# Attention on two 64-row tiles of TensorE: unsplit fp32 scores, transposes in half blocks, a new order

## The chip, the cores and the metric

The kernel runs on one core of a Trainium2 chip. The metric is the device time of one execution in microseconds (us); before the change three runs took 736.19, 736.8 and 738.85 us, median 736.8.

## The reference, cut to what matters

```python
q_rot, k_rot = rotate(q), rotate(k)              # q, k, v: (2 batches, 8 heads, 576, 64), fp32
scores = q_rot @ k_rot.transpose(0, 1, 3, 2) / 8
attn = exp(scores - scores.max(-1))
attn = attn / (attn.sum(-1) + 1e-9)
x = (attn @ v) -> (1152 tokens, 512)
h = x @ w_in                                     # 512 x 2048
g = where(h >= 1, h, where(h <= -1, 0, (h + 1)**2 / 4))
x = g @ w_out                                    # 2048 x 512
p = domain_probs / domain_probs.sum(-1)          # 4 experts
out = sum over e of p[:, e] * (relu(x @ w1[e]) @ w2[e])   # 512 x 1024 x 512 each
```

`rotate` mixes the two 32-column halves of each head with cosines and sines of the position.

## The kernel before, in words

Three parts follow one another: attention, the first MoE layer (products at L654 and L708), the second (L910 and L947). The first layer's products start between the last heads' attention already. The change lies in the attention and in what is shared with it.

*Tiling.* `plan_pair` plans the attention eight times, each time for two heads of one batch. A pair has nine score tiles (`tile_step`): tiles 0 to 7 are a block of 128 queries of one head against that head's 576 keys, the ninth holds the last 64 queries of both heads, one in each half of the partitions.

*Keys and queries.* After the rotation (`rope`, on VectorE or GpSimd) each value x is split in two fp32r numbers, the rounded one h and the difference l (`split_h`, `split_l`). `tr` transposes blocks of 128 positions, h and l side by side, to 128 rows (64 of h, 64 of l); ScalarE copies them to `K1`, `Q1` and, for the ninth tile, `QT`. `K2` is K1 with the halves of the rows swapped, which two DMAs write (`swap`); the first pair has an opening of its own (`k_first`).

*A tile.* A score is Q1 times K1 plus Q1 times K2, for each half of the 576 keys: four matmuls of 288 columns into a two-bank tile `sc` of PSUM (L1300), in the ninth tile eight (L1310). VectorE takes the maximum (L1317), ScalarE the exponential with its sum into `E` (L1322). TensorE transposes four blocks of 128x128 into one bank `pt` (L1335), VectorE or ScalarE copies them to `PT` (L1281, L1283). The last 64 of the 576 keys, of both heads together, are transposed later (`tails`, L1361) and copied to `PU`.

*After four and after all nine tiles* the product with the values follows (`av`, L1411): unsplit fp32, two heads in the two 64-column halves of TensorE's array, five blocks of keys, 256 or 320 queries wide, into a bank of its own. An fp32 product leaves two records in the trace, so that the first four blocks show as x16 and the fifth as x4. Meanwhile the sums' reciprocals are transposed, copied (`rt`) and spread through DRAM by DMA; VectorE multiplies (L1422), and the result is split into `XH` and `XL` for the MoE part.

*PSUM.* Eight banks: two score tiles of two banks, three `pt`, which the transposes of keys and queries share, one `av`.

*What sets the order.* Each engine works through its instructions in the order in which `Plan.order` issues them. That takes the operations from a table, word by word,

```python
table = [self.ops[int(x)] for x in ORDER.split()]
```

and computes for each a start time by planned durations. Where TensorE would be idle for longer than `CFG["fill"]` by these, it inserts "warming" matmuls on a constant (`fill`, L1466), which compute nothing that is used.

Of the kernel before, what the change touches and what calls it, by code (L numbers as in the profile page):

```python
# [28 lines left out]
    "hd": [7, 7, 2, 2], "xd": [0, 3, 2, 2, 0, 3, 3, 2], "r0": 15, "xe": [2, 1, 3, 0, 3, 2, 2, 2], "he": [3, 2, 0, 3, 1, 0, 3, 0], "eb": 3, "rp": [239, 3, 33, 40, 240, 130, 40, 18], "ord0": [0, 1, 3, 5, 2, 4, 6, 7, 8], "ev": 204, "evu": 7, "fill": 272.0, "warm_to": 26000.0, "fill_to": 190000.0, "rule": 1.01, "tc": 190, "rkb": 1, "ahead": 42.6,  # L29
# [17 lines left out]
4 10 3 47 1 2 6 46 48 11 15 16 5 52 17 18 19 50 20 21 49 38 23 29 135 51 54 53 39 24 59 40 60 136 8 9 134 12 143 144  # L47
22 55 33 25 34 56 13 27 137 41 28 26 30 32 145 31 57 58 61 42 149 150 7 35 63 43 62 68 44 64 138 139 0 36 65 163 69 73
37 240 239 241 153 146 74 147 70 78 45 164 154 75 66 157 83 14 869 158 79 80 159 67 88 248 76 81 243 84 89 85 77 86 87
148 151 111 112 93 82 90 141 71 72 249 109 113 242 244 94 114 167 98 140 110 95 345 152 155 156 160 91 99 100 250 103  # L50
168 165 162 104 251 252 870 161 105 166 169 253 117 254 106 124 344 121 142 125 346 92 173 255 170 126 127 115 101 122
123 174 178 175 102 258 96 268 353 259 179 354 180 183 97 262 269 107 181 188 349 263 184 347 264 185 256 176 116 182
193 108 257 348 189 214 177 215 190 171 172 265 216 270 194 198 260 195 118 130 199 271 217 266 261 267 128 129 451
191 218 203 357 355 119 200 186 449 356 358 359 192 120 272 131 204 360 219 132 450 913 246 205 187 208 209 459 196
363 273 373 222 210 871 914 458 211 364 229 220 374 274 454 197 453 226 230 367 278 227 275 221 368 369 460 206 361
228 452 212 362 223 201 279 283 213 207 245 280 231 232 202 556 276 277 284 554 555 233 288 375 370 872 365 285 371
366 462 289 461 293 294 377 464 247 465 234 235 564 224 376 290 875 321 558 295 372 322 463 319 320 298 299 303 873
323 559 324 291 563 325 304 300 281 296 133 305 292 874 297 308 565 286 309 282 287 236 313 301 310 468 478 352 378
479 469 302 314 225 327 876 315 334 237 661 316 335 379 331 336 337 472 557 351 380 383 332 333 326 473 317 306 388
466 474 318 384 467 350 311 381 659 307 567 385 566 382 393 312 475 660 470 480 338 328 476 482 389 477 394 395 238  # L60
877 569 390 339 426 880 340 427 570 398 341 428 471 878 424 662 429 399 481 403 391 430 425 400 404 405 386 396 392
387 408 401 397 413 402 409 432 568 329 410 669 879 418 881 406 342 414 415 416 882 419 407 420 483 583 668 577 584
417 421 578 573 574 579 663 439 330 664 484 571 455 488 436 672 489 437 440 422 438 485 766 490 411 572 493 441 412
670 423 442 431 498 433 494 495 456 671 575 585 580 445 581 587 503 576 499 500 883 884 343 582 764 586 674 673 504
505 529 508 486 530 487 434 496 509 510 491 497 513 514 501 502 675 443 531 444 506 518 532 767 492 511 560 515 533
507 446 534 457 435 512 523 519 535 520 885 516 886 682 683 524 561 517 887 588 589 769 678 525 688 684 676 677 679
537 526 541 689 593 680 544 590 685 681 536 598 542 543 594 545 538 521 687 527 599 595 765 603 522 604 686 596 546
600 528 605 447 448 608 550 888 636 692 609 597 690 637 773 638 613 891 768 610 547 774 614 591 618 691 639 634 619
592 606 611 615 620 635 612 607 775 623 624 779 601 780 628 616 621 625 602 617 626 693 793 629 630 794 622 627 783
777 776 562 778 698 548 549 631 632 784 646 919 920 921 922 694 647 648 699 889 640 641 649 650 633 787 781 695 892  # L70
551 700 789 782 923 916 924 788 797 667 703 701 708 539 702 704 642 925 709 540 705 710 643 713 718 651 739 741 552
652 890 655 714 715 723 716 553 719 740 785 720 696 771 893 894 742 770 717 786 728 711 721 724 725 644 697 722 729
733 712 730 645 743 706 726 744 734 653 790 798 897 654 707 731 735 666 736 791 792 745 727 895 751 752 803 928 929
930 931 799 753 804 800 808 805 665 732 737 813 806 656 772 746 809 932 933 754 934 896 814 747 926 738 810 918 898
899 795 801 807 815 846 796 818 844 823 802 657 935 811 755 756 902 757 748 760 824 812 819 825 749 845 900 820 901
927 847 826 828 827 829 821 816 833 848 822 758 750 759 830 937 817 831 838 938 849 834 835 939 658 940 836 832 903
850 839 840 859 761 904 837 852 860 941 942 943 851 861 841 905 842 853 856 862 946 947 948 908 843 854 855 975 976
977 978 857 949 906 858 865 993 994 995 996 863 907 864 762 909 944 945 950 936 910 951 952 763 979 980 981 866 953
911 954 982 983 867 868 1011 1029 1012 1030 1031 1032 1087 1013 1014 1038 912 1039 917 1101 997 998 999 915 1020 1115
984 985 1040 1041 986 1015 1021 1042 1016 1022 1023 1017 1047 1048 987 1049 1000 1046 1001 1024 1028 1033 1034 1018  # L80
1035 1019 988 1025 1050 1036 1002 989 1003 990 1026 1004 1043 1005 991 1120 992 1006 1125 1027 1044 1088 1089 1007
1037 1076 1102 1008 1103 1045 1009 1116 1051 1117 1010 1056 1121 1057 1090 1077 1052 1104 1091 1058 1118 1105 1053
1122 1119 1059 1067 1054 1078 1068 1055 1069 1060 1070 955 1071 1079 956 1066 1072 957 1061 958 960 1073 959 961 1080
1062 962 1074 1064 963 1075 1086 965 1063 964 966 1065 967 1081 968 1092 1123 1093 970 969 971 1094 1082 972 1095 1084
973 1124 1083 1126 974 1085 1127 1096 1106 1128 1130 1129 1131 1107 1100 1132 1097 1133 1135 1108 1134 1136 1098 1109
1137 1138 1110 1140 1139 1141 1099 1114 1142 1143 1111 1145 1156 1157 1146 1144 1158 1112 1147 1159 1176 1148 1160
1177 1113 1161 1178 1179 1149 1185 1165 1186 1162 1155 1187 1180 1150 1188 1163 1181 1194 1189 1166 1195 1151 1164
1196 1153 1152 1197 1190 1239 1154 1198 1244 1167 1199 1249 1182 1254 1168 1183 1203 1191 1295 1204 1169 1205 1192
1206 1184 1175 1212 1170 1207 1213 1208 1214 1193 1171 1215 1200 1173 1240 1172 1201 1221 1174 1216 1222 1202 1217
# [105 lines left out]


def mm_ns(n):
    return max(86, n / 2.4 + 13.3)


T32, T32R = 109, 87


def act_ns(n, sbuf=False):
    return (93 if sbuf else 51) + 0.833 * n


# [1446 lines left out]
```

## Time and profile before

| | |
|---|---|
| median of three runs | 736.8 us |
| profiled execution | 736.78 us, span 735.0 us |
| TensorE (PE) busy | 726.4 us, 99% of the span |
| VectorE (DVE) busy | 536.5 us, 73% |
| ScalarE (ACT) busy | 351.4 us, 48% |
| GpSimd (POOL) busy | 90.0 us, 12% |
| granted clock of TensorE | 1.00 in all three stretches shown below |

The span is the recorded part of the execution. Busy is the time in which an engine has an instruction in work; matmuls are pipelined, so the records of neighbours overlap, and what a group of matmuls costs is read from the start of the first to the start of what follows.

### The profile page before, as it was taken

How to read it: one execution, taken by the hardware profiler on the slowest of the kernel's cores; microseconds unless marked ns; L12 is line 12 of the kernel's file. 1: busy time of each engine (PE TensorE's matmuls, PEld its weight loads, DVE VectorE, ACT ScalarE, POOL GpSimd, SP SyncE). 2: the span in 40 equal slices, each digit the busy share in tenths (PEclk: the TensorE clock that was granted, in tenths of full speed). 3: DMA queues.
4: the chain of work that ended last, by engine and by line, in shares of the span. 5: the costliest groups of instructions: out<-in, count | busy, mean ns of one | idle time of the engine just before them, and what ended most of it. 6: DMA issues, size and time to landing. Idle time of an engine off the chain costs nothing.

```text
span 735.0 us, 11809 instructions
## 1 busy us (share of the span) xinstructions
PE 726.4 (99%) x4545; PEld 663.3 (90%) x4545; DVE 536.5 (73%) x1054; ACT 351.4 (48%) x802; POOL 90.0 (12%) x88
## 2 busy tenths in 40 slices
PE   8999999999999999999999999999999999999998
PEld 6878788879999999999999988998889988999896
DVE  6789998899999843226898586774867849668462
ACT  4887798867776554335534232431324313333120
POOL 3764415000000112231200000000000000000000
PEclk9999999999999999999999999999999999999999
DMA  4545433325354200000111110111101110011002
GB/s 115 160 120 130 145 87 119 107 82 171 115 175 131 97 1 0 1 1 11 48 55 62 58 57 1 59 58 58 58 1 57 58 58 35 25 58 58 1 29 101
DMA packets 38872, 50.78 MB, mean 69 GB/s; under 512 B 7640, under 2 KB 22560, under 8 KB 38816
## 3 DMA queue, kind: packets, MB, share of 16 engines
q1 hardware_dynamic: 38126, 49.61, 21.9%
q8 instruction: 36, 0.59, 0.3%
q10 hardware_dynamic: 690, 0.41, 0.2%
q14 instruction: 20, 0.16, 0.1%
HBM read 43.26 MB, written 2.40 MB: 62 GB/s over the span
## 4 chain that ended last, share of the span: by engine, by line
PE 93%; DVE 3%; DMA 2%; ACT 1%; SPq 0%; issue 0%; POOL 0%; DVEq 0%; POOLq 0%
PE po L947 27%; PE q L910 23%; PE pi L654 14%; PE po L708 14%; PE av L1411 5%; PE sc L1300 4%; PE pt L1335 4%; PE sc L1310 1%; DMA rawk<-in_k_dram 1%; PE pu L1361 1%; DMA K<-K 1%; DVE tsa L919 1%; PE pstk L1183 1%; PE pstq L1183 1%; ACT E L1322 1%; DMA rbs<-rdram 0%
## 5 line engine op out<-in xcount | busy, mean ns | idle before, releaser
L919 DVE TENSOR_TENSOR tsa<-q,tsa 128x256 f32<-128x256 f32 (+1 forms) x224 | 93.7, 451 | 32.9 <-PE q L910 32.4
L947 PE MATMUL po<-w,ct 128*128 128x512 f32 (+1 forms) x328 | 99.2, 384 | 0.0
L962 DVE SCALAR_TENSOR_TENSOR ACC<-po,ptile,ACC 128x512 f32<-128x512 f32 (+1 forms) x64 | 46.9, 741 | 67.3 <-PE po L947 67.2
L947 PE MATMUL po<-w,hid1h 128*128 128x512 f32 x256 | 79.0, 390 | 0.0
L947 PEld LDWEIGHTS po<-w,ct 128*128 128x128 f32 x328 | 60.5, 188 | 11.7
L947 PE MATMUL po<-w,tsb 128*128 128x512 f32 (+1 forms) x164 | 63.0, 384 | 0.0
L1317 DVE TENSOR_REDUCE nm<-sc 128x1 f32<-128x576 f32 x72 | 53.8, 752 | 7.9 <-PE sc L1300 3.9
L1322 ACT ACTIVATE E<-sc,nm 128x576 f32<-128x576 f32 x72 | 53.6, 746 | 12.0 <-DVE nm L1317 8.9
L947 PEld LDWEIGHTS po<-w,hid1h 128*128 128x128 f32 x256 | 47.6, 188 | 9.4
L675 ACT ACTIVATE hb<-pi,half_t 128x384 f32<-128x384 f32 x48 | 27.7, 578 | 49.4 <-PE pi L654 49.4
L799 ACT CAST w<-wrawa 128x512 fp32r<-128x512 f32 x32 | 18.4, 617 | 67.0 <-PE po L947 64.7
L1300 PE MATMUL sc<-K,Q 128*128 128x288 f32 x256 | 49.3, 315 | 0.9 <-DMA K<-K 0.6
L947 PE MATMUL po<-w,hid1l 128*128 128x512 f32 x128 | 49.9, 390 | 0.0
L893 ACT ACTIVATE ct<-tsa 128x320 fp32r<-128x320 f32 x64 | 29.0, 471 | 42.9 <-DVE tsa L919 42.9
L679 DVE SCALAR_TENSOR_TENSOR hb<-hb,pi 128x384 f32<-128x384 f32 x48 | 26.3, 550 | 27.1 <-ACT hb L677 16.9
L893 ACT ACTIVATE hid1h<-tsa 128x256 fp32r<-128x256 f32 x64 | 25.4, 418 | 37.3 <-DVE tsa L919 37.3
L1335 PE MATMUL pt<-ident,E 128*128 128x128 f32 x288 | 40.1, 274 | 0.5 <-DVE PT L1281 0.3
L1300 PEld LDWEIGHTS sc<-K,Q 128*128 128x128 f32 x256 | 36.0, 188 | 4.7 <-issue 2.2
L922 ACT COPY tsa<-q 128x256 f32<-128x256 f32 (+1 forms) x32 | 12.7, 398 | 52.1 <-PE q L910 52.0
L720 DVE TENSOR_TENSOR ACC<-po,ACC 128x384 f32<-128x384 f32 x36 | 20.0, 555 | 23.9 <-PE po L708 23.9
L947 PEld LDWEIGHTS po<-w,tsb 128*128 128x128 f32 x164 | 30.8, 188 | 6.1
L1335 PEld LDWEIGHTS pt<-ident,E 128*128 128x128 f32 x288 | 33.1, 140 | 2.8 <-ACT E L1322 1.0
(234 smaller groups left out, 1961.4 us busy)
## 6 DMA issues: line engine op xcount, KB each, us to landing
wrawa<-in_moe_w_dram SPq DMA_DIRECT2D x16, 1024.0 KB
wrawa<-in_moe_w_in_dram SPq DMA_DIRECT2D x5, 1024.0 KB
wrawa<-in_moe_w_out_dram SPq DMA_DIRECT2D x5, 1024.0 KB
K<-K SPq DMA_DIRECT2D x14, 304.0 KB
ta<-in_moe_w_in_dram SPq DMA_DIRECT2D x3, 1024.0 KB
ta<-in_moe_w_out_dram SPq DMA_DIRECT2D x3, 1024.0 KB
rawk<-in_k_dram SPq DMA_DIRECT2D x16, 128.0 KB
RV<-in_v_dram SPq DMA_DIRECT2D x16, 128.0 KB
```

Of the source, the lines that this page charges most:

```text
L654: nc.tensor.matmul(ps()[:, 0:384], w[:, kt * P:(kt + 1) * P], x[:, kt, cols], start=(kt == 0 and m == 0), stop=(kt == 3 and m == 2))
L708: nc.tensor.matmul(ps()[:, 0:N], lh, rh, start=(kt == 0 and m == 0), stop=(kt == 3 and m == 2))
L893: op("ACT", act_ns(n, port) + 20, pr, lambda: nc.scalar.activation(hv(0), src(), AF.Relu), rk + gates[0], [hk], bufs, phase=1)
L910: nc.tensor.matmul(ps()[:, 0:n], w[x][:, kt, a * P:(a + 1) * P], r[y][:, kt, :], start=(kt == 0 and m == 0), stop=(kt == 1 and m == 2))
L919: nc.vector.tensor_tensor(ct(a, j), psv(), ct(a, i), op=ALU.add)
L947: nc.tensor.matmul(ps()[:, 0:f1 - f0], x[y], w[z][:, f0:f1], start=(kt == 0 and m == 0), stop=(kt == 3 and m == 2))
L962: op("DVE", 65 + 1.17 * (f1 - f0), pr, lambda acc=acc, ps=ps, t=t, f0=f0, f1=f1: nc.vector.scalar_tensor_tensor(acc(), ps()[:, 0:f1 - f0], ...
L1300: nc.tensor.matmul(sc()[:, a, 0:288], lh, KK()[:, c0:c0 + 288], start=(x == 0), stop=(x == 1))
L1317: op("DVE", 665, g0 + O["max"], lambda: nc.vector.tensor_reduce(nm(), pv(), axis=AX.XY, op=ALU.max, negate=True), [sc], [nm], [sc, nm])
L1322: nc.scalar.activation(Et()[:, o0:o0 + 576].rearrange("p (a c) -> p a c", a=2), pv(), AF.Exp, bias=nm(), scale=1.0, accum_out=sm()[:, s:s ...
L1335: nc.tensor.transpose(ps()[:, t * P:(t + 1) * P], Et()[:, c0 + t * P:c0 + (t + 1) * P], ident)
L1411: nc.tensor.matmul(pa()[64 * j:64 * j + 64, 0:N], lh, rh, start=(t == 0), stop=(t == 4))
```

## The change

*Scores.* Keys and queries are no longer split. A head has 64 dimensions, so a product needs only 64 rows of the array; keys 0 to 287 lie in the upper 64 rows (`KF`), keys 288 to 575 in the lower. A tile is two fp32 matmuls of 288 columns, one with the upper half of the rows into the first bank of `sc`, one with the lower half into the second (L1336); the ninth is four. Queries are needed in both halves of the rows: `QX` holds half of the blocks in each, and `QY`, written by DMA, the halves swapped (the DMA of keys goes). The first pair (`FB`) writes its queries twice instead.

*Transposes.* `turn` transposes a block as two halves of 64 rows, one from the upper rows into the first bank, one from the lower into the second. The target is the score tile itself, once its exponential has been read out. The last 64 keys are a fifth block of the second head's tiles (of both in the ninth); `tails` and `PU` go. So a score tile keeps its banks until its transposes are copied to `PT` (L1374, L1376, L1380). Keys and queries are transposed in the same way, in tiles of the same ring (`psk`, `psq`).

*PSUM.* Three score tiles, and two banks for `av`, the reciprocals' transposes and the MoE's first products; a third bank joins these when the attention is through (`psJ`).

*Waits and engines.* `av` also waits for `rt`. A string of bits (`alt`) says for about 190 operations whether VectorE or its alternative does them: copies on VectorE or ScalarE, rotations and differences on VectorE or GpSimd. VectorE has 9 copies of 512 and 12 of 640 elements of exponentials (32 of 512 before), ScalarE 23 of 512, 20 of 640 and the ninth tiles' seven (40 of 512 before).

*Order.* `ORDER` is a new table. On TensorE the scores are 128 matmuls of 288 columns and 32 on half as many stationary columns (256 and 64 before), the transposes 824 halves (483 full blocks before), the warming matmuls 31 (34), 15 of them after the first score (3); 72 matmuls of the MoE stand ahead of the last av (60).

```diff
 ORDER = """
-4 10 3 47 1 2 6 46 48 11 15 16 5 52 17 18 19 50 20 21 49 38 23 29 135 51 54 53 39 24 59 40 60 136 8 9 134 12 143 144
+4 1 16 0 3 15 17 2 19 18 10 29 28 11 5 20 38 34 30 33 22 24 119 35 39 21 6 31 44 23 7 9 36 114 43 113 32 40 25 8 37 26
...
-    psT = ctx.enter_context(tc.tile_pool(name="psT", bufs=3, space=PSUM))
+    psT = ctx.enter_context(tc.tile_pool(name="psT", bufs=2, space=PSUM))
-    psS = actx.enter_context(tc.tile_pool(name="psS", bufs=2, space=PSUM))
-    psA = actx.enter_context(tc.tile_pool(name="psA", bufs=1, space=PSUM))
+    psS = actx.enter_context(tc.tile_pool(name="psS", bufs=3, space=PSUM))
...
+        def turn(ps, e, t, zs=(0, 1)):
+            for z in zs:
+                r = slice(64 * z, 64 * z + 64)
+                nc.tensor.transpose(ps()[:, z, 64 * e:64 * e + 64], t[r, :], ident[r, r])
...
+        def both(t, e0, e1):
+            return t[:, :, 64 * e0:64 * e1].rearrange("p h (e c) -> p e h c", c=64)
...
+            def tq():
+                for e, z in enumerate((0, 5, 3, 7, 2)):
+                    turn(psq, e, R()[:, 576 + 64 * z:576 + 64 * z + P])
...
+            def swap():
+                for j in range(2):
+                    nc.sync.dma_start(QY()[64 * j:64 * j + 64, 0:640], QX()[64 - 64 * j:128 - 64 * j, 0:640])
...
+        def query(u, j, a):
+            r = slice(64 * a, 64 * a + 64)
...
+            c = (2 * j + u // 2) * P
+            return (QX if u % 2 == a else QY)()[r, c:c + P]
+        def keys(j, a):
+            return KF()[64 * a:64 * a + 64, 320 * j + 32 * a:320 * j + 32 * a + 288]
...
-                def qk():
-                    lh = Q1()[:, j * 512 + i * P:j * 512 + (i + 1) * P]
-                    for a in range(2):
-                        c0 = j * 576 + a * 288
-                        for x, KK in enumerate((K1, K2)):
-                            nc.tensor.matmul(sc()[:, a, 0:288], lh, KK()[:, c0:c0 + 288],
-                                             start=(x == 0), stop=(x == 1))
...
+            def qk():
+                for a in range(2):
+                    for jj in (j,) if s < 8 else (0, 1):
+                        o = sc()[:, a, 0:288] if s < 8 else sc()[64 * jj:64 * jj + 64, a, 0:288]
+                        nc.tensor.matmul(o, query(i, jj, a), keys(jj, a), start=True, stop=True)
...
             def tt():
-                for t in range(4):
-                    nc.tensor.transpose(ps()[:, t * P:(t + 1) * P], Et()[:, c0 + t * P:c0 + (t + 1) * P], ident)
+                for t in range(nb):
...
+                        c = 512 if t == 4 else 640 * j + t * P
+                        turn(sc, t, Et()[:, c:c + P])
...
+                    cp(PT[g]()[:, 4 * j:4 * j + nb, c:c + P].rearrange("p a (h c) -> p a h c", h=2), both(sc(), 0, nb))
...
-            pa = buf("av", f"av{n}{g}")
+            pa = buf("pt", f"av{n}{g}")
...
-            rk = [(PT[g], z) for z in range(lo, hi)] + [(PU[g], 0)]
+            rk = [(PT[g], z) for z in range(lo, hi)] + [rt]
```

Where the second pair's last tiles meet the third pair's first, TensorE had this before (a name is the buffer, with pair and tile: `pt1_5` is tile 5 of pair 1, counted from 0, `av10` pair 1, first product; `hlk3` are the split keys of pair 3):

```order
L1335 MATMUL pt1_5_731<-ident_58,E1_2_608 128x128 x4
L1183 MATMUL pstk3_0_736<-identr_59,hlk3_694 128x128 x4
L1300 MATMUL sc2_0_741<-K1_2_537,Q1_2_653 128x288
L1300 MATMUL sc2_0_741<-K2_2_699,Q1_2_653 128x288
...
L1183 MATMUL pstk3_8_746<-identr_59,hlk3_694 128x128
L1411 MATMUL av10_748<-PT01_590,RV1_94 64x256 x8
L1411 MATMUL av10_748<-PU01_606,RV1_94 64x256 x2
L1361 MATMUL pu1_1_784<-ident_58,E1_2_608 128x128
L1361 MATMUL pu1_1_784<-ident_58,E1_3_684 128x128
L1361 MATMUL pu1_1_784<-ident_58,E1_4_759 128x128
```

and has this now:

```order
L1336 MATMUL sc1_8_683<-KF1_335,QX1_370 64x288 x2
L1336 MATMUL sc1_8_683<-KF1_335,QY1_427 64x288 x2
L1336 MATMUL sc1_7_694<-KF1_335,QY1_427 128x288
L1336 MATMUL sc1_7_694<-KF1_335,QX1_370 128x288
L1336 MATMUL sc2_0_710<-KF2_691,QX2_592 128x288
L1336 MATMUL sc2_0_710<-KF2_691,QY2_616 128x288
L1425 MATMUL av10_716<-PT01_489,RV1_92 64x256 x10
L1362 MATMUL sc1_8_683<-ident_58,E8_90 128x64 x10
L1145 MATMUL sc1_7_694<-ident_58,E1_3_640 128x64 x10
L1403 MATMUL rb11_772<-ident_58,r11_748 5x128
L1145 MATMUL sc2_0_710<-ident_58,E2_0_740 128x64 x8
```

Scores of three tiles now stand together, then one av, then the three tiles' transposes into those same tiles; before, scores, transposes of another tile and transposes of keys alternated.

On ScalarE, shortly ahead of that place, exponentials (L1322) and copies stood in turn:

```order
L1322 ACTIVATE E1_2_608,sum1_499<-sc1_4_566,nm1_4_600 128x576
L1283 COPY PT01_590<-pt1_0_610 128x4x128
L1380 ACTIVATE r10_621<-sum1_499 128x2x2
L1322 ACTIVATE E1_2_608,sum1_499<-sc1_5_592,nm1_5_625 128x576
L1194 ACTIVATE Q1_2_653<-pstq2_8_623 128x128
L1202 ACTIVATE Q1_2_653<-pstq2_4_616 128x384
L1194 ACTIVATE Q1_2_653<-pstq2_0_632 128x512
```

Now they stand there so (L1349 is the exponential, L1374 the copy out of a score tile, `psk2` the transposed keys of pair 2):

```order
L1349 ACTIVATE E1_2_619,sum1_474<-sc1_5_595,nm1_5_613 128x576
L1349 ACTIVATE E1_2_619,sum1_474<-sc1_4_610,nm1_4_632 128x576
L1349 ACTIVATE E1_3_640,sum1_474<-sc1_6_598,nm1_6_635 128x576
L1374 COPY PT11_669<-sc1_5_595 128x5x128
L1374 COPY PT11_669<-sc1_4_610 128x4x128
L1161 COPY KF2_691<-psk2_672 128x256
L1163 COPY KF2_691<-psk2_672 128x64
...
L1349 ACTIVATE E8_90,sum1_474<-sc1_8_683,nm1_8_704 128x576
L1349 ACTIVATE E1_3_640,sum1_474<-sc1_7_694,nm1_7_708 128x576
L1349 ACTIVATE E2_0_740,sum2_741<-sc2_0_710,nm2_0_713 128x576
```

Three exponentials follow one another, then the copies of their tiles; the queries' copies of several sizes have gone from between.

## Rows read from the trace of the kernel before

**Rows 1.** The page: busy by engine (part 1), and the chain by engine (part 4).

```profile
PE 726.4 (99%) x4545; PEld 663.3 (90%) x4545; DVE 536.5 (73%) x1054; ACT 351.4 (48%) x802; POOL 90.0 (12%) x88
...
PE 93%; DVE 3%; DMA 2%; ACT 1%; SPq 0%; issue 0%; POOL 0%; DVEq 0%; POOLq 0%
```

**Rows 2.** Windows: stretch, its us, busy (count) by engine, PEclk, DMA share, GB/s.

```profile
0.00:15.00 15.00, 12.23 (x57) 9.61 (x58) 10.05 (x28) 5.05 (x13) 3.02 (x14) 1.00 0.40 115
15.00:167.20 152.20, 149.93 (x1179) 123.73 (x1178) 134.34 (x272) 124.45 (x350) 60.96 (x49) 1.00 0.43 118
167.20:735.00 567.80, 564.25 (x3312) 529.98 (x3312) 392.07 (x757) 221.86 (x441) 25.98 (x26) 1.00 0.16 55
```

**Rows 3.** Waits of TensorE, 15.0 to 167.2: us in all, times, longest.

```profile
PE pstk L1183 <- POOL hlk L1166: 0.9, 1, 0.9
```

**Rows 4.** Timeline of TensorE: start, us, instructions; 43 to 59, stage's first and last.

```profile
15.00 0.77 PE L1300 MATMUL sc<-K,Q 128*128 128x288 f32 x4
...
43.24 0.78 PE L1300 MATMUL sc<-K,Q 128*128 128x288 f32 x4
43.85 0.60 PE L1335 MATMUL pt<-ident,E 128*128 128x128 f32 x4
44.21 1.31 PE L1310 MATMUL sc<-K,QT 128*128 128x288 f32 x8
45.35 0.60 PE L1335 MATMUL pt<-ident,E 128*128 128x128 f32 x4
45.71 0.54 PE L1183 MATMUL pstk<-identr,hlk 128*128 128x128 f32 x4
46.09 0.76 PE L1300 MATMUL sc<-K,Q 128*128 128x288 f32 x4
...
46.83 1.95 PE L1411 MATMUL av<-PT,RV 128*64 128x256 f32 x16
...
49.14 0.55 PE L1361 MATMUL pu<-ident,E 128*128 128x128 f32 x3
...
50.41 1.47 PE L1335 MATMUL pt<-ident,E 128*128 128x128 f32 x12
51.64 0.77 PE L1300 MATMUL sc<-K,Q 128*128 128x288 f32 x4
...
55.72 2.38 PE L1411 MATMUL av<-PT,RV 128*64 128x320 f32 x16
...
58.56 0.44 PE L1361 MATMUL pu<-ident,E 128*128 128x128 f32 x2
...
166.46 0.71 PE L1411 MATMUL av<-PU,RV 128*64 128x320 f32 x4
```

**Rows 5.** Groups of VectorE by shape, 0 to 175: count, busy us, mean ns, idle before.

```profile
L1281 DVE COPY PT<-pt 128x512 f32<-128x512 f32 x32 | 21.4, 683 | 0.3
L1281 DVE COPY PU<-pu 128x320 f32<-128x320 f32 x8 | 3.9, 490 | 3.1 <-PE pu L1361 3.0
L1281 DVE COPY PU<-pu 128x256 f32<-128x256 f32 x8 | 3.3, 416 | 0.4 <-PE pu L1361 0.4
L1281 DVE COPY PU<-pu 64x64 f32<-64x64 f32 x8 | 1.8, 228 | 0.3
```

**Rows 6.** Groups of ScalarE by shape, 0 to 175.

```profile
L1283 ACT COPY PT<-pt 128x512 f32<-128x512 f32 x40 | 23.2, 587 | 7.2 <-PE pt L1335 7.1
L1188 ACT CAST K<-pstk 128x512 fp32r<-128x512 f32 x14 | 8.0, 583 | 0.1
L1194 ACT ACTIVATE Q<-pstq 128x512 fp32r<-128x512 f32 x8 | 4.8, 595 | 0.3 <-PE pstq L1183 0.2
```

**Rows 7.** Timeline of ScalarE: one exponential and the reading of its sum.

```profile
44.84 0.74 ACT L1322 ACTIVATE E<-sc,nm 128x576 f32<-128x576 f32 x1 [0.25 <-DVE nm L1317]
45.49 0.19 ACT L1322 ACTIVATION_READ_ACCUMULATOR E<-sc,nm 128x1 f32 x1
```

**Rows 8.** Timeline of TensorE in the opening: warming matmuls.

```profile
9.71 1.07 PE L1466 MATMUL warm<-identr 128*128 128x512 f32 x4
```

## What I expected, and why

> **What bounds the kernel now.** I read the page's busy shares and its chain first: TensorE is busy for 726.4 of 735.0 us, and 93% of the chain that ends last is TensorE's own work [rows 1]. Then the busy time by stage [rows 2]. The attention stage lies between 15.0 us, where the first score is issued, and 167.2 us, where the last product with the values ends [rows 4]. In these 152.2 us TensorE is busy 149.9 us, VectorE 134.3 (88%), ScalarE 124.5 (82%); the granted clock is 1.00, which is the upper of the two levels. What TensorE waits for in the stage comes to 2.3 us, and its longest waits are single ones of under 1 us [rows 3]. Behind the stage lie 567.8 us of the two MoE layers, again TensorE from end to end. Their matmuls are the same in number and shape before and after (576 + 576 + 1344 + 876 of the first layer's two products and the second's), so I cost that part at nothing. The start is costed at nothing too: the first score still follows the whole chain of the first pair's rotations on VectorE, some twenty small operations in either kernel. So the change is worth what it takes out of TensorE's stream in the attention stage, less the new gaps it leaves there.
>
> **The terms.** A "busy" of a matmul is no price, because the records of neighbours overlap; I use start to start in the timeline of 16 us in the stage [rows 4].
>
> *Scores.* A score tile of four 288-column matmuls runs from 43.24 to 43.85, 0.61 us, and the eight of the ninth tile from 44.21 to 45.35, 1.14 us. Eight pairs have 64 and 8 of these: 64 x 0.61 + 8 x 1.14 = 48.2 us. After, every tile is two (ninth: four) unsplit fp32 matmuls, which stand in the upper and the lower half of the array's rows and write two banks. No row shows that form. Nearest are the products with the values (av): unsplit fp32 too, two at a time in the two halves of the array's columns, in five steps. They take 46.83 to 49.14 = 2.31 us with 256 columns and 55.72 to 58.56 = 2.84 us with 320. The difference, 0.53 us over 5 x 64 columns, is 1.66 ns for a column of such a double step; what is left of 2.31 us, 0.19 us, is going into and out of the split array. So a score tile costs 288 x 1.66 = 0.48 us if halves of rows run beside each other as halves of columns do, and 0.96 if they don't. I take 0.48, since the av rows show the side-by-side running at these sizes: 72 x 0.48 = 34.4 us, **13.8 us less**.
>
> *Transposes.* Twelve full ones take 50.41 to 51.64, four 45.71 to 46.09: 0.095 us each. Before there are 288 of the exponentials, 40 of their tails and 129 of split keys and queries after 15 us (155 in all, 26 in the opening): 457 x 0.095 = 43.4 us. After, each becomes two half blocks; the tails ride along as a fifth block, and the keys and queries, no longer doubled by the split, need 10 halves each for a pair. That is 796 halves, 398 couples, after the first score. The price of a couple isn't in the trace. Side by side and in proportion to the columns it would be half a full one, 0.0475 us; side by side and at a fixed price for a block, 0.095; one behind the other, 0.19. I take 0.071, between the first two, because the rows lead there: a 288-column matmul of a score takes 0.61 / 4 = 0.1525 us, a 128-column transpose 0.095, so 160 columns cost 0.0575 us, 0.36 ns each, and 0.049 us are left as the fixed part; 64 columns then make 0.072. 398 x 0.071 = 28.3 us, **15.1 us less**.
>
> A rule speaks against it. The trace has 0.095 us for a full block [rows 4], and none for a half. The Trainium skill, page "TensorE: Matmul & The Clock Gate", section "LDWEIGHTS (loading the stationary operand)", says that loading the stationary block takes as long for few rows as for all, since its columns decide; the stationary block of a half transpose keeps its 128 columns. By that rule halving gains nothing as soon as the load decides; this is rival 4.
>
> *Changes between the whole and the split array.* Before, 31 (only av is split); after, 94 from the first score on, since scores and transposes are split one way, av another, and the small transposes of the sums and the MoE's matmuls not at all. At 0.19 / 2 = 0.095 us each, 63 more are **6.0 us more**. The same skill, page "TensorEngine Tiling (Array Packing)", section "Key Properties", has such a change drain the engine; the trace agrees as far as the 0.19 us of av go.
>
> *New waits.* The order now issues three score tiles in a row and their transposes in a row (the first pieces in the section on the change), because a tile's transposes go back into its own two banks and three such tiles are all there are. From a tile's start to the end of its exponential the trace has 43.24 to 45.58, the read of the sum to 45.68 [rows 4, 7]; that is 2.4 us in which TensorE needs other work. With an av (2.3 to 2.8 us) between the scores and the transposes it has it; one batch of three in each pair has none. I put 0.7 us on each of seven pairs, 5.0 us. In the first pair, 15 warming matmuls are placed after the first score where 3 were; they stand where nothing else was ready: 12 more at 0.22 us, from four in 9.71 to about 10.6 [rows 8], 2.6 us. Together **7.6 us more**; the bounds are 0 and 15.
>
> The av also waits now for the transposed sums' copy on ScalarE, and behind it on TensorE stand the next tiles' transposes; the sums' transpose is placed rows ahead of it, so I cost that at nothing, and at up to 0.3 us for each of 16 if it is late (in the bounds above).
>
> *VectorE and ScalarE* must not become the end. VectorE loses the second copies of tails, 3.3 + 3.9 + 1.8 us, the casts and differences of the split, some 7, about 3.4 of weight differences that go to GpSimd, and copies of exponentials (32 of 0.683 become 9 of that size and 12 of 640 elements at 0.82): about 24 us less [rows 5], 110 in the stage. ScalarE gains about 11 us of such copies and of the ninth tile's, and loses about 22 of key and query copies, casts and tails against it [rows 6]: some 114. TensorE is left with 149.9 - 13.8 - 15.1 + 6.0 = 127. So it remains the fullest, but no longer by far.
>
> **Sum:** -13.8 - 15.1 + 6.0 + 7.6 = -15.3 us. The profiled execution took 736.8 us, its span 735.0, and the median of the runs is 736.8 as well; the forecast is 721.5 us.
>
> **Rivals.**
>
> 1. *Half transposes run one behind the other.* Then a couple costs 0.19 us, 47.4 us more than I take, and 5 of the new waits vanish under it: 721.5 + 47.4 - 5 = 764 us, slower. The price decides from 0.071 + 15.3 / 398 = 0.11 us on. For it: no row shows halves of rows at work. Against: av's halves of columns overlap. If the scores ran one behind the other as well, another 34 us. This is the case on the other side.
> 2. *The ring of three score tiles is the bound.* A tile now holds its banks through exponential, transposes and copy. By rows, 2.4 us to the sum, 0.2 and 0.3 for the transposes, 0.6 to 0.7 for the copy: 3.6 us. But in a batch of three the second and third wait their turn for ScalarE, one exponential with its sum (0.85 us by the starts 44.84 and 45.68) more each: about 4.5 on average. With two further uses a pair of 1.5 us each, the stage lasts (72 x 4.5 + 16 x 1.5) / 3 = 116 us, under the 137 of the forecast (152.2 - 15.3). It would be the bound at 5.3 us, and at 6.0 the whole gain is gone. VectorE and ScalarE at above 80% make 5.6 possible: (72 x 5.6 + 24) / 3 = 142, 5 us more than forecast, and a few at the seams between pairs: 729 us.
> 3. *The clock.* TensorE, now waiting more often, falls from 2.4 to 1.2 GHz for part of the stage. For it: gaps of 1 to 2 us in a batch without av. Against: 1.00 in the opening as in the stage, waits included [rows 2]. A quarter of 127 us at half speed costs 32 us: about 753 us.
> 4. *A block's price is fixed.* Two halves side by side cost what one full block does, 0.095 us: 398 x 0.024 = 9.5 us more than I take, 731 us. For it: the fixed part above is already half of a block's price. Against: the other half goes with the columns.
>
> **How the numbers follow.** Forecast 0.51, rival 1 0.12, rival 2 0.14, rival 3 0.09, rival 4 0.14. The forecast's own range, by 0.0475 to 0.085 for a couple (-9 to +6 us), waits of 0 to 15 us, and up to 6 us on scores for loads that aren't covered, is 707 to 735. For 8 in 10, I go down to 704 and up to 741, which takes in rivals 2 and 4 and leaves out rival 1 and most of 3. A measurement of this kernel tells about 0.5% (3.7 us) from no change. Faster: nearly all of the forecast and of rivals 2 and 4, 0.77; same: their upper ends, 0.08; slower: rivals 1 and 3, 0.15.
>
> **What would show it.** In the profile after: the last av ends between 150 and 156 us, not at 167; a score tile start to start near 0.48 us and ten halves near 0.36; TensorE idle 5 to 15 us in the stage, most of it before transposes and released by ScalarE; the granted clock 1.00; the stretch from the last av to the end as long as before, or shorter by the 12 MoE matmuls more that now precede it. A tile at 0.9, ten halves at 0.9, or idle time released by the copies out of the score tile would show rivals 1 or 2 right. The forecast is wrong if the last av ends after 163 us, or if the MoE part grows.

## The result

The changed kernel takes 730.03 us in the median of six runs (726.69 to 730.6), the kernel before 736.36 in six of its own; the ratio is 0.9896 (95% interval 0.987 to 0.9923). That is 6.3 us less where 15.3 less was forecast: inside the range, the right sign, and less than half of the size. The profiled execution took 726.87 us, 9.9 less than that of before. Two of the six runs lie near 727 us and four near 730; what may part them is looked at with e4 and e5, and is not shown for all of them. The steps are first held against the profile.

The page of the changed kernel, parts 1 and 4, to be read beside [rows 1]:

```profile
PE 711.7 (98%) x4883; PEld 622.1 (86%) x4883; DVE 514.6 (71%) x1002; ACT 344.3 (47%) x763; POOL 89.5 (12%) x92
...
PE 90%; DVE 3%; ACT 2%; DMA 2%; SPq 1%; issue 1%; POOL 0%; DVEq 0%; POOLq 0%; ACTq 0%
```

Its windows, cut at the first score and behind the last av, columns as in [rows 2]:

```profile
0.00:10.76 10.76, 8.40 (x45) 5.40 (x46) 6.21 (x23) 4.31 (x13) 1.51 (x13) 1.00 0.47 129
10.76:158.90 148.14, 140.69 (x1546) 88.64 (x1542) 114.67 (x222) 119.08 (x313) 61.03 (x53) 1.00 0.39 109
158.90:725.10 566.20, 562.60 (x3302) 528.10 (x3300) 393.78 (x759) 220.90 (x439) 26.96 (x26) 1.00 0.16 55
```

The stage is only 4 us shorter (148.1 for 152.1, which is 15.00 to 167.10 by the starts; [rows 2] cut 0.1 us later), but begins 4.2 us earlier; behind it 566.2 us are left for 567.9, since 12 more MoE matmuls stand ahead. VectorE and ScalarE come to 115 and 119 us, 5 us more each than worked out (110, 114). TensorE's timeline in and around the second pair, to be read beside [rows 4]:

```profile
29.16 2.38 PE L1425 MATMUL av<-PT,RV 128*64 128x256 f32 x20
31.47 1.09 PE L1145 MATMUL sc<-ident,E 64*128 64x64 f32 x28
32.49 0.38 PE L1403 MATMUL rb<-ident,r 128*5 128x128 f32 x2
32.80 0.53 PE L1145 MATMUL psq<-ident,R 64*128 64x64 f32 x10
33.16 0.51 PE L1336 MATMUL sc<-KF,QX 64*128 64x288 f32 x1
...
34.82 2.91 PE L1425 MATMUL av<-PT,RV 128*64 128x320 f32 x20
37.66 0.53 PE L1145 MATMUL sc<-ident,E 64*128 64x64 f32 x10
...
49.56 0.47 PE L1145 MATMUL sc<-ident,E 64*128 64x64 f32 x10
49.87 0.46 PE L1336 MATMUL sc<-KF,QX 64*128 64x288 f32 x1
...
50.51 2.91 PE L1425 MATMUL av<-PT,RV 128*64 128x320 f32 x20
...
156.05 2.91 PE L1425 MATMUL av<-PT,RV 128*64 128x320 f32 x20
```

28 halves take 31.47 to 32.49, ten 32.80 to 33.16: 0.073 us a couple (forecast 0.071). Three score tiles ahead of an av take 33.16 to 34.82 = 1.66, so 0.55 each with the change into av; a batch of one takes 0.64 (49.87 to the av at 50.51), so each further tile costs 0.51 (forecast 0.48). Both prices hold. What doesn't is the time between. A batch of three tiles that has no av behind its scores, on TensorE:

```profile
45.17 0.51 PE L1336 MATMUL sc<-KF,QY 64*128 64x288 f32 x1
...
46.39 0.51 PE L1336 MATMUL sc<-KF,QX 64*128 64x288 f32 x1
...
47.66 0.46 PE L1145 MATMUL sc<-ident,E 64*128 64x64 f32 x8 [0.52 <-ACT E L1349]
48.38 0.53 PE L1145 MATMUL sc<-ident,E 64*128 64x64 f32 x10 [0.26 <-ACT E L1349]
```

and ScalarE in the same place, where L1374 is the copy that frees an older score tile:

```profile
45.76 0.57 ACT L1374 COPY PT<-sc 128x512 f32<-128x512 f32 x1
46.77 0.74 ACT L1349 ACTIVATE E<-sc,nm 128x576 f32<-128x576 f32 x1 [0.44 <-DVE nm L1344]
47.41 0.19 ACT L1349 ACTIVATION_READ_ACCUMULATOR E<-sc,nm 128x1 f32 x1
47.50 0.73 ACT L1349 ACTIVATE E<-sc,nm 128x576 f32<-128x576 f32 x1
```

The first tile starts at 45.17, its maximum follows, its exponential ends at 47.5 and its transposes start at 47.66: 2.5 us after the tile's start, of which the matmuls of the three tiles fill 1.5 (3 x 0.51). The third tile, at 46.39, also starts only when the copy of 45.76 has ended at 46.33: the ring of three has no tile to spare. Such waits stand only in part in the list of waits, for this stage:

```profile
PE sc L1145 <- ACT E L1349: 3.6, 10, 0.7
PE sc L1362 <- ACT E L1349: 0.8, 2, 0.6
PE sc L1336 <- ACT PT L1380: 0.7, 2, 0.4
```

so the rest is found by pricing: what the prices don't cover is put down to waits and warming, and an error in a price lands there too. Before: 48.2 for scores, 43.4 for transposes, 41.2 for sixteen av (8 x 2.31 + 8 x 2.84), 1.6 for the sums, 10.8 for 60 MoE matmuls (starts); of 152.1 there remain 6.9. After: 72 x 0.51 = 36.7, 398 x 0.073 = 29.1, 41.2, 3.0, 13.7 for 72 MoE matmuls, and 3.1 for changes at scores (16 x 0.13 into av, 33 batches x 0.03 behind something else); of 148.1 there remain 21.3.

| step, us | forecast | profile |
|---|---|---|
| first score earlier | 0 | -4.2 |
| scores | -13.8 | -11.5 |
| transposes | -15.1 | -14.3 |
| changes whole/split (scores 3.1, sums 1.4) | +6.0 | +4.5 |
| waits and warming (the remainder) | +7.6 | +14.4 |
| 12 MoE matmuls moved ahead | 0 | +2.9 - 1.7 |
| sum | -15.3 | -9.9 |

### The profile page after: what moved, and what is told of

Same layout as the page of the kernel before. It is cut to its first block, busy times and chain, and to the rows that moved or that the text cites. A ratio compares the mean times of both kernels' runs of the same rounds, so it can differ in the third digit from the quotient of the medians.

```text
span 725.1 us, 12366 instructions
## 1 busy us (share of the span) xinstructions
PE 711.7 (98%) x4883; PEld 622.1 (86%) x4883; DVE 514.6 (71%) x1002; ACT 344.3 (47%) x763; POOL 89.5 (12%) x92
## 4 chain that ended last, share of the span: by engine, by line
PE 90%; DVE 3%; ACT 2%; DMA 2%; SPq 1%; issue 1%; POOL 0%; DVEq 0%; POOLq 0%; ACTq 0%
PE pj L958 27%; PE q L921 23%; PE po L719 14%; PE pj L665 12%; PE av L1425 4%; PE sc L1336 4%; PE pi L665 2%; PE sc L1145 2%; ACT E L1349 1%; PE warm L1478 1%; DMA rbs<-rdram 1%; DMA rdram<-rt 1%; DVE tsa L930 1%; DVE nm L1344 1%; SPq L1411 1%
## 5 line engine op out<-in xcount | busy, mean ns | idle before, releaser
L958 PE MATMUL pj<-w,ct 128*128 128x512 f32 (+1 forms) x328 | 99.2, 384 | 0.0
L973 DVE SCALAR_TENSOR_TENSOR ACC<-pj,ptile,ACC 128x512 f32<-128x512 f32 (+1 forms) x64 | 46.9, 741 | 67.3 <-PE pj L958 67.2
L958 PE MATMUL pj<-w,hid1h 128*128 128x512 f32 x256 | 79.0, 390 | 0.0
L958 PEld LDWEIGHTS pj<-w,ct 128*128 128x128 f32 x328 | 60.5, 188 | 11.7
L958 PE MATMUL pj<-w,tsb 128*128 128x512 f32 (+1 forms) x164 | 63.0, 384 | 0.0
L1344 DVE TENSOR_REDUCE nm<-sc 128x1 f32<-128x576 f32 x72 | 51.5, 752 | 13.7 <-PE sc L1336 12.9
L1349 ACT ACTIVATE E<-sc,nm 128x576 f32<-128x576 f32 x72 | 52.7, 738 | 13.9 <-DVE nm L1344 13.5
L958 PEld LDWEIGHTS pj<-w,hid1h 128*128 128x128 f32 x256 | 47.6, 188 | 9.4
L810 ACT CAST w<-wrawa 128x512 fp32r<-128x512 f32 x32 | 18.4, 617 | 67.5 <-PE pj L958 64.7
L958 PE MATMUL pj<-w,hid1l 128*128 128x512 f32 x128 | 49.9, 390 | 0.0
L1336 PE MATMUL sc<-KF,QX 64*128 64x288 f32 (+1 forms) x172 | 45.8, 432 | 1.3 <-ACT KF L1163 0.4
L904 ACT ACTIVATE hid1h<-tsa 128x256 fp32r<-128x256 f32 x64 | 25.4, 418 | 36.7 <-DVE tsa L930 36.6
L1425 PE MATMUL av<-PT,RV 128*64 128x256 f32 (+1 forms) x320 | 42.3, 411 | 0.0
L1336 PE MATMUL sc<-KF,QY 64*128 64x288 f32 (+1 forms) x140 | 40.2, 432 | 0.5 <-ACT PT L1380 0.4
L690 DVE SCALAR_TENSOR_TENSOR hb<-hb,pj 128x384 f32<-128x384 f32 x40 | 22.0, 551 | 24.5 <-ACT hb L688 14.3
```

What stands on the lines that cost most here:

```text
L904: op("ACT", act_ns(n, port) + 20, pr, lambda: nc.scalar.activation(hv(0), src(), AF.Relu), rk + gates[0], [hk], bufs, phase=1)
L958: nc.tensor.matmul(ps()[:, 0:f1 - f0], x[y], w[z][:, f0:f1], start=(kt == 0 and m == 0), stop=(kt == 3 and m == 2))
L973: op("DVE", 65 + 1.17 * (f1 - f0), pr, lambda acc=acc, ps=ps, t=t, f0=f0, f1=f1: nc.vector.scalar_tensor_tensor(acc(), ps()[:, 0:f1 - f0], ...
L1336: nc.tensor.matmul(o, query(i, jj, a), keys(jj, a), start=True, stop=True)
L1344: op("DVE", 665, g0 + O["max"], lambda: nc.vector.tensor_reduce(nm(), pv(), axis=AX.XY, op=ALU.max, negate=True), [sc], [nm], [sc, nm])
L1349: nc.scalar.activation(o.rearrange("p (a c) -> p a c", a=2), pv(), AF.Exp, bias=nm(), scale=1.0, accum_out=sm()[:, s:s + 1])
```

## The experiments

Every variant is the changed kernel with the edit shown; "longer" and "shorter" are against its 730.03 us where nothing else is said.

**e1, whole blocks instead of halves.**

```diff
-                        turn(sc, t, Et()[:, c:c + P])
+                        nc.tensor.transpose(sc().rearrange("p a b -> p (a b)")[:, t * P:(t + 1) * P], Et()[:, c:c + P], ident)
...
-                    cp(PT[g]()[:, 4 * j:4 * j + nb, c:c + P].rearrange("p a (h c) -> p a h c", h=2), both(sc(), 0, nb))
+                    cp(PT[g]()[:, 4 * j:4 * j + nb, c:c + P], sc().rearrange("p a b -> p (a b)")[:, 0:nb * P].rearrange("p (a c) -> p a c", c=P))
```

> The changed kernel with the transposes of exponentials (first eight tiles) as whole 128x128 blocks into the score tile's banks instead of two half blocks; copies as wide as before, all else the same. 288 couples become 288 full blocks. If a couple costs 0.071 us against 0.095 for a full block and TensorE's stream sets the end: +6.9 us, and ten halves (0.36 us in the changed kernel) become five blocks of 0.48. If a block's price is fixed (rival 4 of the prediction): 0. If the chain from score to exponential sets the end of a batch: under 3 us. More changes between whole and split array could add up to 5.

738.68 us, 8.7 longer (against before: ratio 1.0021, 1.0008 to 1.0033). A batch of three, behind an av, in its timeline:

```profile
35.58 1.75 PE L1365 MATMUL sc<-ident,E 128*128 128x128 f32 x14
37.17 0.38 PE L1403 MATMUL rb<-ident,r 128*5 128x128 f32 x2
```

14 blocks take 1.59 us for 1.02 as halves. 14 x 0.095 would be 1.33. What the other 0.26 is stays open: it isn't a change between whole and split, since here an av stands ahead and a whole matmul (`rb`) behind, so that the halves change twice and the blocks once. Halving pays, and rival 4 (fixed price of a block) falls.

**e9, all upper halves, then all lower** (with the 16 warming matmuls of e5, to compare with e5).

```diff
-                for t in range(nb):
+                for z, t in [(z, t) for z in (0, 1) for t in range(nb)] if s < 8 else []:
+                    turn(sc, t, Et()[:, c:c + P], (z,))
```

> e5_warm6 (728.2 us) with the half transposes of tiles 1 to 8 issued all upper halves first, then all lower halves. If halves run beside each other only where upper and lower alternate: ten halves take 0.48 to 0.95 us instead of 0.36, and the kernel gets 7 to 25 us longer. If a half costs the same wherever it stands: no change, under 1 us.

729.53 us, 1.3 longer than e5. In its timeline, again a batch of three:

```profile
33.18 1.21 PE L1145 MATMUL sc<-ident,E 64*128 64x64 f32 x28
34.32 0.38 PE L1406 MATMUL rb<-ident,r 128*5 128x128 f32 x2
```

28 halves, four or five of the same rows in a row, take 1.14 us for 1.02: 0.081 a couple. Lying side by side gives 0.008 of it (288 couples, 2.3 us); the rest comes with the half itself, which has 64 rows and 64 columns where a block has 128 of each; no run separates the two. My number was right, half of my reason wasn't: halves that share their rows cost 0.081 a couple and not 0.19, and rival 1 was no danger.

**e2, both score matmuls in the upper rows.**

```diff
-                        nc.tensor.matmul(o, query(i, jj, a), keys(jj, a), start=True, stop=True)
+                        nc.tensor.matmul(o, query(i, jj, 0), keys(jj, 0), start=True, stop=True)
```

> The changed kernel with both matmuls of a score tile in the upper half of the array's rows (the second 288 scores are computed from the first 288 keys, so the scores are not the reference's). If the halves run beside each other now, a tile goes from 0.49 us to about 0.96 and the kernel gets 25 to 34 us longer when TensorE's stream sets the end, 15 to 25 when its waits (7.8 us idle, 5.4 of warming in the stage) cover part. If the halves already run one behind the other: no change.

779.65 us (one of four runs 768.9), 49.6 longer, more than any case said. Two tiles and what follows them, in its timeline:

```profile
100.57 1.24 PE L1336 MATMUL sc<-KF,QY 64*128 64x288 f32 x4
101.64 1.13 PE L1336 MATMUL sc<-KF,QX 64*128 64x288 f32 x4
102.42 0.60 PE L1145 MATMUL sc<-ident,E 64*128 64x64 f32 x8
```

A tile takes 1.85 / 2 = 0.93 us for 0.51, so scores do run side by side, and 72 x 0.42 = 30 us are explained. The rest lies ahead of the end of the first av, where TensorE ran at about half its rate:

```profile
6.90 0.55 PE L1145 MATMUL psk<-ident,first 64*128 64x64 f32 x5 [0.61 <-DVE first L1220]
...
39.25 0.80 PE L1145 MATMUL sc<-ident,E 64*128 64x64 f32 x10
39.84 1.27 PE L1336 MATMUL sc<-KF,QX 64*128 64x288 f32 x2
...
56.37 4.53 PE L1425 MATMUL av<-PT,RV 128*64 128x256 f32 x20
60.84 1.48 PE L1145 MATMUL sc<-ident,E 64*128 64x64 f32 x28
```

The first five transposes last 0.55 us by their record (0.37 in the changed kernel's profile), ten halves take 39.25 to 39.84 = 0.59 us for 0.36, and the first av 56.37 to 60.84 = 4.47 us for 2.31, though the granted clock is recorded as 1.00 all the while. This av ends 29.4 us later than the changed kernel's (60.84 for 31.47), of which 13 tiles at 0.42 are 5.5; about 24 us are the rate. Behind it the profiled execution (779.48 us for 726.87) loses another 23 us over 59 tiles, 0.39 each, which is the price of the scores again. So this run shows two things at once, and the scores account for 30 us of it.

**e3, the maximum over half of the keys.**

```diff
-nc.vector.tensor_reduce(nm(), pv(), axis=AX.XY, op=ALU.max, negate=True)
+nc.vector.tensor_reduce(nm(), sc()[:, 0, 0:288], axis=AX.X, op=ALU.max, negate=True)
```

> The changed kernel with the maximum taken over the first 288 of the 576 scores (the exponentials are shifted by that instead; the quotient is the same). VectorE has 72 x about 0.33 us less, and each tile's exponential may start 0.33 us sooner. If the batches of three wait for the chain score, maximum, exponential: 4 to 9 us shorter, and the idle time before the transposes (4.5 us in the stage) falls to about half. If TensorE's own stream sets the end: 0 to 2 us shorter.

727.86 us, 2.2 shorter. **e7, half of the exponentials in pairs 3 to 8** (with e5's warming):

```diff
+                if n >= 2:
+                    nc.scalar.activation(o[:, 0:288], sc()[:, 0, 0:288], AF.Exp,
+                                         bias=nm(), scale=1.0, accum_out=sm()[:, s:s + 1])
+                    return
```

> e5_warm6 (728.2 us) with the exponential of pairs 3 to 8 over 288 of the 576 scores only; the other half of E is left as it was. ScalarE has 54 x about 0.3 us = 16 us less to do, and each of these tiles' transposes may start up to 0.3 us sooner (0.9 for the third of a batch). If TensorE waits for the chain score, maximum, exponential: 5 to 12 us shorter, idle before transposes under 2 us. If the ring of three tiles or TensorE's own stream sets the end: 0 to 3 us shorter.

725.53 us, 2.7 shorter than e5. TensorE's waits for exponentials (transposes of tiles 1 to 8, from the second pair's end on) fall from 3.6 us to 2.0 in e3, and from e5's 3.1 to 1.8 in e7, yet e3's 2.2 us lies between its two cases, and e7's 2.7 us in the case that I had set for the ring or TensorE's own stream (0 to 3). Part of the 2.7 is the clock: three of e5's four runs have a mean granted clock of 0.997 or 0.998, all of e7's 0.999 or 1.000, and e5's one run at 1.00 took 726.62 us, 1.1 more than e7. A step of the chain that is 0.33 us shorter saves 1 to 3 us, not 24 batches x 3 x 0.33. That fits batches that wait once, for their first tile, and only where no av follows the scores.

**e8, the copies out of the score tiles twice in pairs 3 to 8** (with e5's warming).

```diff
+                    for _ in range(2 if n >= 2 else 1):
                         cp(PT[g]()[:, 4 * j:4 * j + nb, c:c + P].rearrange("p a (h c) -> p a h c", h=2), both(sc(), 0, nb))
```

> e5_warm6 (728.2 us) with the copies out of the score tiles done twice over in pairs 3 to 8: 48 copies of 0.6 to 0.8 us more, about two thirds on ScalarE, and each of these tiles holds its banks that much longer. If the ring of three tiles is what TensorE waits for (rival 2 of the prediction): 48 x 0.67 / 3 = 11 us longer or more. If ScalarE's load is: 15 to 22 us longer. If TensorE's stream alone sets the end and the two engines have room: 0 to 5 us longer.

752.83 us, 24.6 longer than e5: above what the load or TensorE's stream alone would give, and within the "11 or more" of the ring. The waits of TensorE in the stage:

```profile
PE sc L1336 <- ACT PT L1375: 8.8, 16, 0.7
PE psq L1145 <- DVE PT L1375: 2.1, 2, 1.1
```

Scores and transposes of keys and queries now wait for the copies that free a tile, 14.6 us in all such rows of the view (0.6 in e5), while ScalarE itself still waits for transposes (11.0 us) and for the maximum (9.2). So the waits speak for the ring rather than ScalarE's load. The size doesn't tell them apart, for the 24.6 us are not all copies: the granted clock fell in this run too, in the profiled execution from 75 to 80 us and several times from 140 to 165; the deepest stretch is

```profile
145.00:150.00 5.00, 5.00 (x34) 2.76 (x36) 1.99 (x4) 2.90 (x7) 0.00 (x0) 0.50 0.32 82
```

A mean clock of 0.991 over 751 us is up to 6.8 us of TensorE's time (an estimate; it is less where TensorE would have waited). That leaves 18 to 25 us for 48 copies of about 0.67 us, 0.37 to 0.5 each: near the 15 to 22 that I had set for the load as well, and more than the third that a ring of three with tiles evenly in work would pass on.

**e4, no warming after the first score.**

```diff
-"fill_to": 190000.0
+"fill_to": 10000.0
```

> The changed kernel without the 15 warming matmuls after the first score. If they fill gaps only: 0 to 2 us shorter, and the same stretch (10.8 to 28 us) shows idle time instead. If they hold up what stands behind them: 3 to 5 us shorter. If they keep the clock up: the granted clock falls below 1.00 in the first pair and the kernel gets 3 us or more longer.

729.21 us, 0.8 shorter. The time in which TensorE is not busy in the stage rises from 7.5 to 11.3 us, where 5.4 us of warming went: it had filled gaps. Windows of this execution,

```profile
5.00:10.00 5.00, 3.17 (x18) 1.61 (x18) 4.80 (x18) 1.71 (x9) 0.00 (x0) 0.81 0.40 114
10.00:15.00 5.00, 5.00 (x29) 3.19 (x31) 2.13 (x6) 1.80 (x6) 2.38 (x2) 0.51 0.64 173
```

and of the changed kernel's profiled one, which has the same opening up to there:

```profile
5.00:10.00 5.00, 4.31 (x29) 2.25 (x27) 5.00 (x18) 2.35 (x11) 0.00 (x0) 1.00 0.43 119
10.00:15.00 5.00, 4.96 (x48) 2.92 (x46) 4.46 (x8) 3.73 (x10) 2.83 (x2) 1.00 0.67 201
```

In e4 TensorE paused 1.8 us after the ten first warming matmuls (0.7 in the other); the first line is e4's, the second the changed kernel's:

```profile
7.37 0.37 PE L1145 MATMUL psk<-ident,first 64*128 64x64 f32 x5 [1.76 <-DVE first L1220]
...
6.99 0.37 PE L1145 MATMUL psk<-ident,first 64*128 64x64 f32 x5 [0.69 <-DVE first L1220]
```

The granted clock (last but two of the columns) was at the lower level from about 8 to about 15 us, and the first score came at 13.19 instead of 10.76. e3's profile shows the same (0.80, 0.52; 13.14), and e1's, behind a pause of 1.0, a fall to 0.50 from 10 to 15. The last av starts 2.6 us later in e4 (158.64 for 156.05), so this opening costs about what lies between 727 and 730. That it parts the changed kernel's runs is shown for one at most: of the four near 730 one has a mean granted clock of 0.993, the other three 0.999 to 1.000, as the two near 727 have. Nor does the pause alone decide: in e2 it was 0.61 us, and the first transposes behind it already took half as long again as these (0.55 us).

**e5 and e6, 16 and 24 warming matmuls at the start instead of 10.**

```diff
+        if not warmed:
+            cnt += 6
+        warmed.append(1)
...
+    warmed = []
```

> The changed kernel with 16 instead of 10 warming matmuls at the very start. The changed kernel's runs lie at two levels, 726.7 to 726.9 and 729.6 to 730.6; where the first transposes followed the warming after 0.69 us, TensorE ran at full rate and the first score came at 10.8 us, where they followed after 1.0 to 1.7 us (the two variants with a later input) the same transposes take 0.58 instead of 0.40 us from 8 or 9 us on and the first score comes at 12.0 to 13.2. If that pause costs the clock: all runs at 726 to 728, first score by 11.3 us. If the levels come from elsewhere: as many runs near 730 as before.

> As e5_warm6 with 24 warming matmuls at the start, 14 more than the changed kernel. If the pause costs the clock: all runs at one level, but the first transposes are held up by up to 1.8 us against e5_warm6, so 727 to 729. If the pause doesn't matter: 2 us longer than the changed kernel at both levels.

e5: 728.24 us (726.62 to 728.71), 1.8 shorter; the first score at 11.58. Its windows:

```profile
5.00:10.00 5.00, 5.00 (x30) 3.32 (x28) 5.00 (x18) 1.54 (x9) 0.00 (x0) 1.00 0.39 107
10.00:15.00 5.00, 5.00 (x40) 2.72 (x42) 3.62 (x7) 3.72 (x12) 2.82 (x2) 1.00 0.70 207
```

The fall is gone from the opening, but both limits that I set are missed: two of four runs lie above 728, and the first score comes after 11.3. The same execution has a fall later in the stage, behind gaps of TensorE:

```profile
130.00:135.00 5.00, 3.88 (x52) 1.93 (x48) 2.75 (x7) 3.14 (x9) 0.48 (x1) 1.00 0.29 73
135.00:140.00 5.00, 4.66 (x35) 2.97 (x37) 3.69 (x9) 3.92 (x13) 3.17 (x6) 0.66 0.33 96
```

e6 (14 for the 6) and e10 fall there too (0.77 and 0.82 in the same five us). So it isn't only the opening that costs the clock. e6: 729.68 us, first score at 12.43, above the 727 to 729 that I expected if the pause costs the clock, with runs from 728.18 to 730.95 that are no single level; its time fits the other case about as well (2 us longer than the changed kernel at both levels). More warming holds up the start. The first transposes start at 7.83 in e5 and at 8.69 in e6, at 6.99 in the changed kernel's profile.

**e10 and e11, e3 with one warming run at the start (20, then 14) and none after** (the edits of e3, e4 and e5, with 10 and 4 for the 6, and this):

```diff
-                if ok and cnt > 0:
+                if ok and cnt > 0 and not out_warm:
+                    out_warm.append(1)
```

> The changed kernel with the maximum over 288 scores (e3), 20 warming matmuls at the start and no others. The six between the first transposes go, about 0.22 us each. If they stand in the way of the first score: it comes at 10.5 to 11.5 us, and the kernel takes 724 to 726 us, under e3 and e5. If the clock falls without them: the first pair shows transposes of ten at 0.58 us and the time is 728 or more.

> e10_combined with 14 instead of 20 warming matmuls at the start. In e10_combined the first transposes came at 8.95 us, though their input is there at about 7.4. If these six matmuls only held up the opening: the first score at 10.3 to 10.9 us, 724 to 725.2 us in the median. If the pauses that are left then cost the clock: transposes of ten halves at 0.58 us in the opening, first score at 12 us or later, 726 us or more.

e10: 725.75 us, as expected, with the first score at 11.66, just outside the 10.5 to 11.5 that I had set. e11: 724.81 us (723.53 to 726.2), ratio to before 0.9839 (0.9821 to 0.9858), to the changed kernel 5.2 us less: the best version, with the limit that exponentials shifted by the maximum of half the keys are safe only where scores spread little. The opening in its timeline:

```profile
1.66 6.19 PE L1483 MATMUL warm<-identr 128*128 128x512 f32 x14 [1.66 <-DVE identr L1466]
7.78 0.66 PE L1147 MATMUL psk<-ident,first 64*128 64x64 f32 x10
...
10.90 3.19 PE L1338 MATMUL sc<-KF,QX 64*128 64x288 f32 x12
13.83 1.19 PE L1147 MATMUL sc<-ident,E 64*128 64x64 f32 x16
```

The first score comes at 10.90 as expected, but the three first tiles take 2.93 us (1.86 in the changed kernel), at a granted clock of 0.66 from 10 to 15 us. TensorE had gaps of 0.3 to 0.6 us between the transposes just before; but e10 had some of 0.4 and 0.5 there and kept 1.00, so that these gaps alone don't explain the fall. With one warming run at the start the two take 2 to 3 us less than e3 in the median, though their ranges overlap e3's (725.65 to 729.0).

## Why the prediction was right in its direction, and short in its size

- *Scores*: right. 0.51 for 0.48 a tile, and e2's rows at full rate (0.93) show that the two halves of the rows are what makes it.
- *Transposes*: right in size (0.073 for 0.071), wrong in half of the reason (e9). In part this was luck: the forecast had 0.049 us of fixed time in a couple and two halves beside each other, while a half among others of the same rows costs 0.041 in all. The price before was read low, too: the twelve blocks at 50.41 [rows 4] take 0.103 us each and only the four at 45.71 take 0.095, so the 457 may have cost up to 3.4 us more, and the remainder before that much less. The rule from the Trainium skill, "TensorE: Matmul & The Clock Gate", section "LDWEIGHTS (loading the stationary operand)", agrees with the load's own record, below: 139 ns for a half block, 140 for a full one in the kernel before. But the load didn't decide: a half costs 0.036 us from start to start, a full block 0.095.

```profile
L1335 PEld LDWEIGHTS pt<-ident,E 128*128 128x128 f32 x288 | 33.1, 140 | 2.8 <-ACT E L1322 1.0 <-DVE PT L1281 0.8 <-DVE PU L1281 0.4
...
L1145 PEld LDWEIGHTS sc<-ident,E 64*128 64x128 f32 x576 | 21.8, 139 | 16.3 <-ACT E L1349 12.1 <-issue 2.2 <-ACT ha L692 0.4
```

- *Changes whole/split*: 4.5 for 6.0, by 0.13 us into an av and 0.03 elsewhere, where the forecast took 0.095 for each.
- *New waits*: the step that failed. The forecast put +7.6 on "New waits" (0.7 us on each of seven batches, 2.6 of warming); the profile has +14.4. Of the 21.3 us there now, about 7.5 lie in the first pair (5.4 of them warming: 15 matmuls at 0.36 us, most of them alone, where the forecast took 0.22) and about 9 in the batches without av, some 1.0 us each and not 0.7; some 5 are spread in pieces under 0.5. These are remainders by price; what the runs give back of them is less (e3 and e7, 1 to 3 us). What I had left out is that such a batch pays twice: for the chain score, maximum, exponential (e3, e7), and at its third tile for the copy that frees a tile (the rows at 46.39; e8). I had named both, the one as a term and the other as rival 2, but treated them as alternatives. Waits under the records' overlap don't show as idle time (7.5 of 21.3 us do), so that the view of waits alone would have hidden most of it.
- *The first pair*: costed at nothing in the opening, where the change gained. The split's casts and differences went from the chain to the first score, and it came 4.2 us sooner; but the first av of the stage begins at 29.16 against 28.98 us, so what TensorE saved there became warming and waits. What held the pair isn't shown: from 10.76 to 29.16 VectorE is busy 14.4 us and ScalarE 14.2 of 18.4.
- *The clock*, rival 3: I argued against it with "1.00 in the opening" [rows 2]. Before, 29 warming matmuls run up to the first transposes; now 10 do, and a pause of 0.6 to 1.8 us follows. The argument didn't carry over: the clock fell in the opening of e1, e3, e4 and e11, and later in the stage in e5, e6, e8 and e10, if for far less than the quarter of the stage that rival 3 was priced at. A fall in the opening costs some 2.5 us (e4), and that may be the 3.2 us between the profiled run, which has none, and the median; but three of the four runs near 730 show none in their mean clock, so that this part of the 8.5 us between forecast and median stays open. e5, made to remove it, gets back 1.8.

That the MoE part costs the same was right (566.2 + about 2 for the moved matmuls against 567.9), and so was that neither VectorE nor ScalarE becomes the end by its load.

## What to carry to other kernels

When an engine that was 99% busy gets cheaper instructions, price the gaps of the new stream, not only its instructions: for each batch, the chain through the other engines and the release of its buffers, together. A gain in work shows in the total only where what TensorE waits for comes sooner too; in the first pair here it didn't. And where an opening is shortened, look at the granted clock in several executions, and at the time of an instruction that you know.

## What the runs showed of the hardware

- A transposed half block (64 rows, 64 columns out) costs 0.036 us, 38% of a full one, and hardly more (0.041) if its neighbours stand in the same rows.
- Unsplit fp32 matmuls of 288 columns in the two halves of the rows run nearly fully beside each other: 0.51 us for two, 0.93 when both stand in one half.
- The record of the granted clock doesn't show every slow stretch: in e2 it is 1.00 where the same ten halves take 0.59 us instead of 0.36, and an av 4.47 instead of 2.31.
- A pause of 1.8 us in the opening, where another execution had 0.7, was followed by 7 us at the lower clock level, and the first score came 2.4 us later; in e2 the same transposes were slow behind a pause of 0.6, so the length of the pause doesn't settle it.
